# Softmax with tokens on partitions, turned by DMA, in a fused attention and bilinear FFN

## The chip, the cores and the metric

The kernel runs on one core of a Trainium2 chip. The metric is the device time in microseconds of one execution, the median of several. The core has five engines that this text names: TensorE (PE, matmuls), VectorE (DVE), ScalarE (ACT), GpSimd (POOL) and SyncE (SP), which here only issues DMAs. Each engine works through its own queue in order and waits on semaphores. DMAs issued by SP and those issued by GpSimd have queues of their own.

## What is computed

Eight batches of eight heads, 576 tokens (S), head dimension 64 (D), 32 memories (M) in each head:

```
a      = softmax(phi) over the 576 tokens' 32 memories      # [tokens, 32] of each head
k_m    = a.T @ k ;  v_m = a.T @ v                           # 32 x 64 means, each head
attn   = softmax(q @ k_m.T / 8) over the 32 memories        # [tokens, 32]
x      = attn @ v_m, heads side by side                     # [4608, 512]
out    = ((x @ w_a) * (x @ w_b)) @ w_out                    # d_ff = 1536, out [4608, 512] f32
```

The kernel leaves out maxima, folds `v_m` into `w_a` and `w_b` for each batch (`vab`), so that `attn` is the direct input of the up products, and works in f16 with f32 sums in PSUM. In place of dividing `a` by its sums it divides the means by sums taken with a column of ones.

## The kernel before, in words

Work is cut by batch. A batch has 12 blocks of d_ff (128 each) and two halves of 288 tokens. An *up step* for block `i` and half `hf` (`up_half`, L598) is two matmuls into a PSUM tile `pa` and two into `pb`, both with `attn[b]` (tile A, heads times memories on partitions, tokens along the row) as the moving side; ACT copies `pa` to `a_sb` (L609), DVE multiplies it with `pb` into `ht` (L612). The *down products* (`two_downs`, L464) take two blocks of 128 tokens at once by a scheme with seven products in place of eight, from sums of `ht` that GpSimd makes (`sum_tokens`, L455), into PSUM tiles `py`, `pv`, `px`; ACT and DVE finish them into `o_sb` (four buffers), and SP stores them.

The order is written out by hand. `ups` runs through the up steps and after each pulls some down products from a common list, at a rate that `Work.plan` sets from what is ready, and then runs one *slot* of a plan: names of units of the next batch, separated by blanks, several in one slot joined by `+`. A prime stands for the batch after that one, `_` for the one before. `d3` pulls three products at once, `L` starts the loads of a later batch on GpSimd's queue. The main loop (L703 to L710) takes batches b = 2 to 7; each has two halves of 12 slots, and the plan of its slots treats batch b + 1: `second` for b = 2, `every` for 3 to 5, `last` for 6. In this text "the loop of batch 4" is b = 4, in which batch 5's attention is made.

The units of a batch:
- `exp0`, `exp1`: exponential of phi (ACT).
- `kv`, `km` (or `km0`, `km1`): the sums with k, v and ones on TensorE into two PSUM tiles `pkv`, and their scaling into `rep` (`take_kv`, L233).
- `kvt` or `kvd`: turning `rep` into `kvT`, by six TensorE transposes and a DVE copy (`kv_transpose`, L241), or by one DMA transpose that SP issues (`kv_turn`, L247). Batches 2 to 4 use the first, 5 to 7 the second.
- `qt0` to `qt3`: turning the query in 32x32 blocks of f32 pairs on DVE (`q_transpose`, L203). The contraction over D is then split in even and odd columns, and each tile of TensorE has 32 rows.
- `sc`, `e0`, `e1`: scores (L297, memories on partitions) and their exponential into E (L310).
- `den0`, `den1`: sums over memories, a matmul with a block matrix of ones into `pD` (L320), and their logarithm L (ACT, L321).
- `nr0`, `nr1`: R = exp(-L) (ACT, L329) and A = E * R (GpSimd, L331).
- `v0` to `v2`, `x0a` to `x2b`: folds of the means into the weights (`fold`, L343) and their copies out of PSUM (`take_fold`, L355).

PSUM has eight banks. `Banks` hands them out in turn; tiles taken with `hold=True` (scores, folds, `py`, `pv`, `px`, `pkv`) keep theirs until freed, the others go round. Tiles of the pools `mid` and `inp` (E, A, qT, kvT, the query) have two buffers.

Of the kernel before, what the change touches and what calls it, by code (L numbers as in the profile page):

```python
# [18 lines left out]
def kernel(  # L19
# [26 lines left out]
    mid = ctx.enter_context(tc.tile_pool(name="mid", bufs=2))  # L46
    small = ctx.enter_context(tc.tile_pool(name="small", bufs=2))
# [25 lines left out]
    phis, qs, kvs = {}, {}, {}  # L73
# [71 lines left out]
    banks = Banks()  # L145
# [31 lines left out]

    attn = {}
    vabs = {}

    def head(g, j):

        jj = j ^ g
        return jj % 2, 2 * g + jj // 2

    def units(b):

        u = {}
        t = {}
# [10 lines left out]
        def q_transpose(hp):  # L200
            if hp == 0:
                t["qT"] = mid.tile([P, NHP, NI * D], F16, name="qT")
            nc.vector.transpose(out=t["qT"][:, hp, :].bitcast(F32), in_=qs[b][:, hp, :].bitcast(F32))  # L203

        def kv_sums():

            t["pkv"] = [banks.take([P, 3, D], F32, "pkv", hold=True) for _ in range(2)]
            for i in range(NI):
                for g in range(2):
                    for j in range(4):  # L210
                        r, hp = head(g, j)
                        nc.tensor.matmul(  # L212
                            t["pkv"][g][0][32 * j:32 * j + 32],
                            t["exp"][64 * r:64 * r + 64, hp, i, :],
                            kvs[b][64 * r:64 * r + 64, :, hp, D * i:D * (i + 1)],
                            start=(i == 0),
                            stop=(i == NI - 1),
                            tile_position=(64 * r, 32 * j),
                        )

        def take_kv(gs=range(2)):

            if gs[0] == 0:
                t["rep"] = mid.tile([P, 6, P], F16, name="rep")
                t["rphi"] = small.tile([P, 2], F32, name="rphi")
            for g in gs:
                pkv, bank = t["pkv"][g]
                nc.vector.reciprocal(out=t["rphi"][:, g:g + 1], in_=pkv[:, 2, 0:1])
                km = pkv[:, 0].rearrange("p (d e) -> p e d", e=2).unsqueeze(2).to_broadcast([P, 2, 4, 32])
                vm = pkv[:, 1].unsqueeze(1).to_broadcast([P, 2, D])  # L230
                for out, x in ((t["rep"][:, 2 * g:2 * g + 2].rearrange("p e (z d) -> p e z d", z=4), km),
                               (t["rep"][:, 4 + g].rearrange("p (z d) -> p z d", z=2), vm)):
                    nc.vector.tensor_scalar(out=out, in0=x, scalar1=t["rphi"][:, g:g + 1], scalar2=None, op0=ALU.mult)  # L233
                banks.free(bank)

# [8 lines left out]
        def kv_turn():  # L244

            t["kvT"] = mid.tile([P, 6, P], F16, name="kvT")
            nc.sync.dma_start_transpose(out=t["kvT"], in_=t["rep"].rearrange("p x d -> p (x d)"))  # L247

        def sums(g, x):

# [32 lines left out]
        def scores(gs):  # L283
# [7 lines left out]
            for dh in range(2):  # L291
                for z in range(2):
                    for g in gs:
                        for j in range(4):
# [8 lines left out]
                                tile_position=(row, 32 * j),  # L303
                            )

        def exp_scores(g):
            Ev = t["E"].rearrange("p g (i z s) -> p g i z s", z=2, s=32)
            for z in range(2):
                pss, bank = t["pss", g][z]
                nc.scalar.activation(out=Ev[:, g, :, z, :], in_=pss, func=AF.Exp, scale=1.0 / (8.0 * CS))  # L310
                banks.free(bank)
# [11 lines left out]
        def normalise(g, hfs=slice(0, 2)):  # L323
# [6 lines left out]
            engine = nc.vector if b < 2 else nc.gpsimd  # L330
            engine.tensor_tensor(out=attn[b][:, g, sl], in0=t["E"][:, g, sl], in1=t["R", g][:, sl], op=ALU.mult)  # L331

        def fold(lo, hi, zs):
            if b not in vabs:
                vabs[b] = [mid.tile([P, 2, d_ff], F16, name=f"vab{x}") for x in range(2)]
            if len(zs) > 1 and b > 2:
                work.settle()
            for z in zs:
                t["pva", lo, z] = [banks.take([P, 512], F32, "pva", hold=True) for _ in range(2)]
                for j in range(4):  # L340
                    for g in range(2):
                        r, hp = head(g, j)
                        nc.tensor.matmul(  # L343
                            t["pva", lo, z][g][0][32 * j:32 * j + 32, 0:hi - lo],
                            t["kvT"][64 * r:64 * r + 64, 4 + g, M * j:M * j + M],
                            w_sbs[z][64 * r:64 * r + 64, hp, lo:hi],
                            start=True,
                            stop=True,
                            tile_position=(64 * r, 32 * j),
                        )  # L350
# [7 lines left out]
        def one(f, *a):  # L358
            return lambda: f(*a)

        for z in range(2):
            u[f"exp{z}"] = one(exp_phi, z)
            u[f"ks{z}"] = one(sums, z, 0)
            u[f"kt{z}"] = one(transpose, z, 0)
            u[f"vs{z}"] = one(sums, z, 1)
            u[f"vt{z}"] = one(transpose, z, 1)
            u[f"s{z}"] = one(scores, (z,))
            u[f"e{z}"] = one(exp_scores, z)
            u[f"km{z}"] = one(take_kv, (z,))
            u[f"den{z}"] = one(denominators, z)  # L370
            u[f"nr{z}"] = one(normalise, z)
            for hf in range(2):
                u[f"den{z}{hf}"] = one(denominators, z, (hf,))
                u[f"nr{z}{hf}"] = one(normalise, z, slice(hf, hf + 1))
            for n in range(NCH):
                u[f"v{n}{'ab'[z]}"] = one(fold, 512 * n, 512 * (n + 1), (z,))
                u[f"x{n}{'ab'[z]}"] = one(take_fold, 512 * n, 512 * (n + 1), z)
            for n in range(2):
                u[f"hv{n}{'ab'[z]}"] = one(fold, 256 * n, 256 * (n + 1), (z,))
                u[f"hx{n}{'ab'[z]}"] = one(take_fold, 256 * n, 256 * (n + 1), z)  # L380
        for n in range(NCH):
            u[f"v{n}"] = one(fold, 512 * n, 512 * (n + 1), (0, 1))
        for x in range(4):
            u[f"qt{x}"] = one(q_transpose, x)
        u["sc"] = one(scores, (0, 1))
        u["kv"] = one(kv_sums)
        u["km"] = one(take_kv)
        u["kvt"] = one(kv_transpose)
        u["kvd"] = one(kv_turn)
        u["-"] = lambda: None  # L390
        return u
# [201 lines left out]
    work = Work()  # L593
# [57 lines left out]
    def slots(b, names):  # L651

        def both(fs):
            return lambda: [f() for f in fs]
        def unit(n):
            if n == "fin":
                return lambda: work.pull(-work.done % NFF)
            if n == "L":
                return lambda: load(b + 2) if b + 2 < B else None
            if n[0] == "y":  # L660
                return lambda: some(int(n[1:]))
            if n[0] == "d" and n[1:].isdigit():
# [34 lines left out]
    ups(half_steps(1, 0, 4), slots(1, "- v2a+x2a+v2b+x2b+qt0' - - qt1'+exp0' exp1'+qt2' - kv'+km'+y9"))  # L697
    work.plan(S + HALF, 10)
    ups(half_steps(1, 1, 4), slots(2, "qt3 kvt - sc+e0+e1 - den0+den1+nr0 - v0+nr1+x0a x0b - v1+x1b x1a"))
    second = "v2_+d1+x2a_+exp0 x2b_ exp1 - kv+km+d2 qt0 d4+kvt+qt1 - qt2+qt3+sc+e0 - e1+v0+d2+x0a+x0b den0+d3 exp0' v1+nr0+x1a x1b+qt0' L+d5 den1 v2+x2a exp1'+qt1'+x2b - - qt2'+kv'+nr1+km' - - qt3'+kvt'+d5"  # L700
    every = "- sc+e0 e1 den0 nr0+v0+x0a+x0b - - exp0' exp1' - v1+x1b+x1a+kv'+km0'+d3 - den1+km1' kvd'+qt0' - - nr1+qt1' v2+x2a+x2b - qt2' - qt3' - - L"
    last = "sc+e0 d3 - e1 v0+x0b - - den1 - - den0+d1 x0a+v1+x1b x1a+nr0 - - - v2+x2a - nr1 - - - - x2b"
    for b in range(2, B):  # L703
        if b == 2:
            load(4)
# [35 lines left out]
```

The softmax here doesn't subtract the row's maximum and nothing guards it: scores larger than these inputs give would overflow.

## Time and profile before

| | us |
|---|---|
| median of 3 runs | 241.4 (241.38 to 241.75) |
| the profiled execution | 241.3 |
| its span, first to last instruction | 239.6 |
| granted TensorE clock, mean | 0.997 |

The first 24 us or so are loading and the first batch; the loop of batch 2 begins at about 72 us, those of batches 4 and 5 at about 126 and 154, and after the last up step only down products are left.

The page's slices cut the span in 40 equal parts; a digit is the busy share in tenths:

```profile
PE   7958999999999999999999999999999999999993
DVE  4636784469949878966975659775976585756642
ACT  2266671669698599687776867797776877465330
POOL 7953244499979629981799948984769087937001
DMA  6999999999967954992359945599130303032155
```

The groups of instructions that the change touches (line, engine, operation, out<-in, shapes and count; then busy us and mean ns of one; then the idle time before them and what ended it):

```profile
L331 POOL TENSOR_TENSOR A<-E,R 128x576 f16<-128x576 f16 x12 | 15.3, 1278 | 4.3 <-ACT R L329 4.3
L310 ACT ACTIVATE E<-pscore 128x288 f16<-128x288 f32 x32 | 11.4, 419 | 11.4 <-PE pscore L297 11.2
L321 ACT ACTIVATE L<-pD 128x288 f32<-128x288 f32 x32 | 11.5, 418 | 6.0 <-PE pD L320 5.8
L203 DVE STREAM_TRANSPOSE qT<-q_sb 128x288 f32<-128x288 f32 x32 | 14.6, 464 | 0.3 <-DMA q_sb<-in_q_dram 0.3
L329 ACT ACTIVATE R<-L 128x576 f16<-128x576 f32 x14 | 9.8, 702 | 0.1
L233 DVE TENSOR_SCALAR rep<-pkv,rphi 128x256 f16<-128x256 f32 x12 | 5.8, 484 | 0.4
L233 DVE TENSOR_SCALAR rep<-pkv,rphi 128x128 f16<-128x128 f32 x12 | 4.1, 342 | 0.0
L455 POOL TENSOR_TENSOR h_sums<-ht 128x768 f16<-128x768 f16 x28 | 46.0, 1644 | 33.9 <-DVE ht L612 33.7
```

### The profile page before, as it was taken

How to read it: one execution, taken by the hardware profiler on the slowest of the kernel's cores; microseconds unless marked ns; L12 is line 12 of the kernel's file. 1: busy time of each engine (PE TensorE's matmuls, PEld its weight loads, DVE VectorE, ACT ScalarE, POOL GpSimd, SP SyncE). 2: the span in 40 equal slices, each digit the busy share in tenths (PEclk: the TensorE clock that was granted, in tenths of full speed). 3: DMA queues.
4: the chain of work that ended last, by engine and by line, in shares of the span. 5: the costliest groups of instructions: out<-in, count | busy, mean ns of one | idle time of the engine just before them, and what ended most of it. 6: DMA issues, size and time to landing. Idle time of an engine off the chain costs nothing.

```text
span 239.6 us, 7764 instructions
## 1 busy us (share of the span) xinstructions
PE 230.6 (96%) x3092; PEld 170.3 (71%) x3092; DVE 165.4 (69%) x403; ACT 158.7 (66%) x410; POOL 159.5 (67%) x135
## 2 busy tenths in 40 slices
PE   7958999999999999999999999999999999999993
PEld 7734664456757867878787787878787778888882
DVE  4636784469949878966975659775976585756642
ACT  2266671669698599687776867797776877465330
POOL 7953244499979629981799948984769087937001
PEclk9999999999999999999999999999999999999998
DMA  6999999999967954992359945599130303032155
GB/s 230 239 197 207 206 258 206 252 213 279 224 154 161 214 115 98 222 208 49 43 123 233 211 90 65 141 212 191 41 85 11 81 16 74 10 83 61 38 130 125
DMA packets 28164, 34.71 MB, mean 145 GB/s; under 512 B 4416, under 2 KB 22208, under 8 KB 28128
## 3 DMA queue, kind: packets, MB, share of 16 engines
q0 software_dynamic: 19264, 23.14, 52.2%
q1 hardware_dynamic: 8352, 10.29, 18.4%
q10 hardware_dynamic: 512, 0.79, 1.0%
q8 instruction: 24, 0.39, 0.7%
q14 instruction: 12, 0.10, 0.1%
HBM read 42.47 MB, written 9.44 MB: 217 GB/s over the span
## 4 chain that ended last, share of the span: by engine, by line
PE 77%; DMA 16%; DVE 2%; issue 1%; POOL 1%; ACT 1%; DVEq 0%; POOLq 0%
PE py L473 18%; PE pa L601 18%; PE pb L601 17%; PE pv L473 9%; DMA wb_sb<-in_moe_w_b_dram 6%; DMA q_sb<-in_q_dram 5%; PE pva L343 5%; DMA kv_sb<-in_v_dram 4%; PE px L473 4%; PE po L398 2%; PE pkv L212 2%; PE pscore L297 1%; PE pD L320 1%; DVE ht L612 1%; ACT a_sb L609 1%
## 5 line engine op out<-in xcount | busy, mean ns | idle before, releaser
L612 DVE TENSOR_TENSOR ht<-a_sb,pb 128x288 f16<-128x288 f16 x168 | 73.3, 450 | 37.5 <-ACT a_sb L609 26.8
L601 PEld LDWEIGHTS <-vab 128*128 128x128 f16 x768 | 72.4, 98 | 24.9 <-issue 7.8
L609 ACT CAST a_sb<-pa 128x288 f16<-128x288 f32 x168 | 66.7, 407 | 25.7 <-PE pa L601 24.6
L601 PE MATMUL pa<-A,vab 128*128 128x288 f16 x384 | 75.8, 287 | 0.1
L601 PE MATMUL pb<-A,vab 128*128 128x288 f16 x384 | 75.0, 286 | 0.7 <-ACT vab L355 0.5
L455 POOL TENSOR_TENSOR h_sums<-ht 128x768 f16<-128x768 f16 x28 | 46.0, 1644 | 33.9 <-DVE ht L612 33.7
L473 PEld LDWEIGHTS <-h_sums 128*128 128x128 f16 x384 | 37.0, 98 | 7.7 <-issue 1.1
L355 DVE CAST vab<-pva 128x512 f16<-128x512 f32 (+1 forms) x52 | 32.3, 644 | 4.8 <-PE pva L343 4.2
L355 ACT CAST vab<-pva 128x512 f16<-128x512 f32 (+1 forms) x52 | 27.7, 569 | 7.8 <-PE pva L343 7.2
L473 PEld LDWEIGHTS <-ht 128*128 128x128 f16 x288 | 28.1, 98 | 5.7 <-issue 0.4
L473 PE MATMUL py<-w_sums,h_sums 128*128 128x256 f16 x192 | 31.3, 273 | 0.0
L455 POOL TENSOR_TENSOR h_sums<-h_sums,ht 128x768 f16<-128x768 f16 x14 | 23.0, 1640 | 1.0
L455 POOL TENSOR_TENSOR h_sums<-ht,h_sums 128x768 f16<-128x768 f16 x14 | 23.0, 1642 | 0.9
L310 ACT ACTIVATE E<-pscore 128x288 f16<-128x288 f32 x32 | 11.4, 419 | 11.4 <-PE pscore L297 11.2
L331 POOL TENSOR_TENSOR A<-E,R 128x576 f16<-128x576 f16 x12 | 15.3, 1278 | 4.3 <-ACT R L329 4.3
L473 PE MATMUL py<-wo_sb,ht 128*128 128x256 f16 x96 | 16.7, 273 | 0.0
L473 PE MATMUL pv<-w_sums,h_sums 128*128 128x256 f16 x96 | 16.5, 273 | 0.0
L473 PE MATMUL py<-w_sums,ht 128*128 128x256 f16 x96 | 15.9, 272 | 0.1
L473 PE MATMUL px<-wo_sb,ht 128*128 128x256 f16 x96 | 15.9, 273 | 0.0
L321 ACT ACTIVATE L<-pD 128x288 f32<-128x288 f32 x32 | 11.5, 418 | 6.0 <-PE pD L320 5.8
L480 ACT ACTIVATE u<-py 128x256 f32<-128x256 f32 x32 | 12.5, 390 | 4.3 <-PE py L473 3.7
L203 DVE STREAM_TRANSPOSE qT<-q_sb 128x288 f32<-128x288 f32 x32 | 14.6, 464 | 0.3 <-DMA q_sb<-in_q_dram 0.3
(65 smaller groups left out, 275.7 us busy)
## 6 DMA issues: line engine op xcount, KB each, us to landing
out_dram<-o_sb SPq DMA_DIRECT2D x68, 128.0 KB, 2.4
phi_sb<-in_phi_dram POOLq DMA_DIRECT2D x8, 576.0 KB, 5.4
kv_sb<-in_v_dram POOLq DMA_DIRECT2D x7, 576.0 KB, 10.3
kv_sb<-in_k_dram POOLq DMA_DIRECT2D x7, 576.0 KB, 6.6
q_sb<-in_q_dram POOLq DMA_DIRECT2D x6, 576.0 KB, 13.1
wo_sb<-in_moe_w_out_dram POOLq DMA_DIRECT2D x6, 256.0 KB, 13.7
q_sb<-in_q_dram POOLq DMA_DIRECT2D x4, 288.0 KB, 9.7
wa_sb<-in_moe_w_a_dram POOLq DMA_DIRECT2D x2, 512.0 KB, 13.8
```

The source lines that it names most:

```text
L203: nc.vector.transpose(out=t["qT"][:, hp, :].bitcast(F32), in_=qs[b][:, hp, :].bitcast(F32))
L310: nc.scalar.activation(out=Ev[:, g, :, z, :], in_=pss, func=AF.Exp, scale=1.0 / (8.0 * CS))
L321: nc.scalar.activation(out=t["L", g][:, sl], in_=pD, func=AF.Ln)
L331: engine.tensor_tensor(out=attn[b][:, g, sl], in0=t["E"][:, g, sl], in1=t["R", g][:, sl], op=ALU.mult)
L343: nc.tensor.matmul(t["pva", lo, z][g][0][32 * j:32 * j + 32, 0:hi - lo], t["kvT"][64 * r:64 * r + 64, 4 + g, M * j:M * j + M], w_sbs[z][64 ...
L355: engine_copy(out=vabs[b][z][:, g, lo:hi], in_=pva[:, 0:hi - lo])
L455: engine.tensor_tensor(out=out, in0=in0, in1=in1, op=op)
L473: nc.tensor.matmul(po, lhs[:, i], rhs[:, i], start=first and i == 0, stop=i == KH - 1, skip_group_check=not first)
L480: nc.scalar.mul(out=x, in_=po, mul=scale)
L601: nc.tensor.matmul(ps, vabs[b][x][:, g, P * i:P * (i + 1)], attn[b][:, g, HALF * hf:HALF * (hf + 1)], start=(g == 0), stop=(g == 1))
L609: nc.scalar.copy(out=a_sbs[b, i, hf], in_=ps)
L612: nc.vector.tensor_tensor(out=ht[:, i, t0:t0 + HALF], in0=a_sbs.pop((b, i, hf)), in1=ps, op=ALU.mult)
```

## The change

For batches from `TURNED` = 3 on, the query is turned by one DMA transpose that SP issues (`q_turn`, 18 blocks of 128x128, f16), and the scores (`token_scores`) contract over all 64 columns of D in one matmul, on tiles of 64 rows: 16 matmuls in place of 32. `take_kv` writes keys and values of a group side by side with one scaling instead of two, and `kv_turn` turns four blocks instead of six; batches 3 and 4 use it now too.

For batches 4 to 7 the softmax over memories is done with tokens on partitions: SP turns E by a DMA transpose (`e_turn`, 9 blocks), DVE sums each run of 32 memories and takes the reciprocal (`token_sums`, in two parts of 640 and 512 columns), GpSimd multiplies the first part and DVE the second (`token_normalise`), and SP turns the result back into A (`a_turn`). The units `den` and `nr` of these batches go. Batch 3 keeps them.

The three plans are written anew.

```diff
+    TURNED = 3
+        def q_turn():
+            t["qT"] = mid.tile([P, NHP, NI * D], F16, name="qT")
+            nc.sync.dma_start_transpose(out=t["qT"].rearrange("p c f -> p (c f)").rearrange("p (n x) -> p n x", x=P),
+                                        in_=qs[b].rearrange("p c f -> p (c f)"))
...
+                if b >= TURNED:
+                    parts = ((t["rep"][:, 2 * g:2 * g + 2].rearrange("p x (z d) -> p x z d", z=2),
+                              pkv[:, 0:2].unsqueeze(2).to_broadcast([P, 2, 2, D])),)
...
-            nc.sync.dma_start_transpose(out=t["kvT"], in_=t["rep"].rearrange("p x d -> p (x d)"))
+            n = 4 if b >= TURNED else 6
+            nc.sync.dma_start_transpose(out=t["kvT"][:, 0:n], in_=t["rep"][:, 0:n].rearrange("p x d -> p (x d)"))
...
+        def token_scores():
...
+                t["pss", g] = [banks.take([P, 5 - y, 64], F32, "pscore", hold=True) for y in range(2)]
+            for g in range(2):
+                for x in range(2):
+                    for j in range(4):
+                        r, hp = head(g, j)
+                        y = (hp + x) % 2
+                        n = (NI * hp + y) // 2
+                        nc.tensor.matmul(
+                            t["pss", g][y][0][32 * j:32 * j + 32],
+                            t["kvT"][64 * x:64 * x + 64, 2 * g, M * j:M * j + M],
+                            qTv[64 * x:64 * x + 64, n:n + 5 - y, 64 * r:64 * r + 64],
+                            start=True,
+                            stop=True,
+                            tile_position=(64 * x, 32 * j),
+                        )
...
+        def e_turn():
+            t["ET"] = mid.tile([P, 2, S], F16, name="E").rearrange("p g s -> p (g s)").rearrange("p (n x) -> p n x", x=P)
+            nc.sync.dma_start_transpose(out=t["ET"], in_=t["E"].rearrange("p g s -> p (g s)"))
...
+            nc.vector.tensor_reduce(out=out, in_=blocks(x), axis=mybir.AxisListType.X, op=ALU.add)
+            nc.vector.reciprocal(out=out, in_=out)
...
+            engine = (nc.gpsimd, nc.vector)[x]
+            engine.tensor_tensor(out=blocks(x), in0=blocks(x), in1=sums.unsqueeze(2).to_broadcast(list(blocks(x).shape)),
+                                 op=ALU.mult)
+
+        def a_turn():
+            attn[b] = mid.tile([P, 2, S], F16, name="A")
+            nc.sync.dma_start_transpose(out=attn[b].rearrange("p g s -> p (g s)").rearrange("p (n x) -> p n x", x=P),
+                                        in_=t["ET"].rearrange("p n x -> p (n x)"))
...
-                            t["kvT"][64 * r:64 * r + 64, 4 + g, M * j:M * j + M],
+                            t["kvT"][64 * r:64 * r + 64, 2 * g + 1 if b >= TURNED else 4 + g, M * j:M * j + M],
...
-    second = "v2_+d1+x2a_+exp0 x2b_ exp1 - kv+km+d2 qt0 d4+kvt+qt1 - qt2+qt3+sc+e0 - e1+v0+d2+x0a+x0b den0+d3 exp0' v1+nr0+x1a x1b+qt0' L+d5 den1 v2+x2a exp1'+qt1'+x2b - - qt2'+kv'+nr1+km' - - qt3'+kvt'+d5"
-    every = "- sc+e0 e1 den0 nr0+v0+x0a+x0b - - exp0' exp1' - v1+x1b+x1a+kv'+km0'+d3 - den1+km1' kvd'+qt0' - - nr1+qt1' v2+x2a+x2b - qt2' - qt3' - - L"
-    last = "sc+e0 d3 - e1 v0+x0b - - den1 - - den0+d1 x0a+v1+x1b x1a+nr0 - - - v2+x2a - nr1 - - - - x2b"
+    second = "v2_+d1+exp0+x2a_ exp1+d6+x2b_ qd+kv+km0+km1+kvd - - d4 - - sc+e0 - e1+d3+v0+d2+x0a+x0b den0 - v1+nr0+x1a x1b+qd' L+exp0'+d5 - v2+x2a exp1'+x2b - - kv'+den1+nr1+km' kvd' - d7"
+    every = "sc+e0+e1+d3+ed+d3 - - v0+x0a+x0b - sm0 sm1 - tn1+exp0' d5+tn0+exp1' ad v1+x1b+x1a+kv'+km0' qd'+km1' kvd' - - v2+x2b - - - - - L+x2a"
+    last = "sc+e0+e1+ed - - v0+x0b+d5 - - sm0+d4 tn0 sm1+d5 tn1 x0a+v1+x1a+x1b - ad - - v2+x2a - - - d4 - x2b"
```

`qd`, `ed` and `ad` are the three turns, `sm` the sums and `tn` the normalisation by parts.

More of the change, by code (lines that the diff above doesn't have):

```diff
@@ L230, in take_kv @@
                 vm = pkv[:, 1].unsqueeze(1).to_broadcast([P, 2, D])
-                for out, x in ((t["rep"][:, 2 * g:2 * g + 2].rearrange("p e (z d) -> p e z d", z=4), km),
-                               (t["rep"][:, 4 + g].rearrange("p (z d) -> p z d", z=2), vm)):
+                parts = ((t["rep"][:, 2 * g:2 * g + 2].rearrange("p e (z d) -> p e z d", z=4), km),
+                         (t["rep"][:, 4 + g].rearrange("p (z d) -> p z d", z=2), vm))
+                if b >= TURNED:
+                    parts = ((t["rep"][:, 2 * g:2 * g + 2].rearrange("p x (z d) -> p x z d", z=2),
+                              pkv[:, 0:2].unsqueeze(2).to_broadcast([P, 2, 2, D])),)
+                for out, x in parts:
                     nc.vector.tensor_scalar(out=out, in0=x, scalar1=t["rphi"][:, g:g + 1], scalar2=None, op0=ALU.mult)
@@ L304, in scores, with token_exp_scores @@
                             )
+        def token_scores():
+            t["E"] = mid.tile([P, 2, S], F16, name="E")
+            work.settle()
+            qTv = t["qT"].rearrange("p c f -> p (c f)").rearrange("p (n x) -> p n x", x=P)
+            for g in range(2):
+                t["pss", g] = [banks.take([P, 5 - y, 64], F32, "pscore", hold=True) for y in range(2)]
+            for g in range(2):
+                for x in range(2):
[11 more added lines that the diff above has]
+                        )
+        def token_exp_scores(g):
+            Ev = t["E"].rearrange("p g (i s) -> p g i s", s=64)
+            for y in range(2):
+                pss, bank = t["pss", g][y]
+                nc.scalar.activation(out=Ev[:, g, y::2, :], in_=pss, func=AF.Exp, scale=1.0 / (8.0 * CS))
+                banks.free(bank)
         def exp_scores(g):
@@ L331, in normalise, with blocks, token_sums, token_normalise @@
             engine.tensor_tensor(out=attn[b][:, g, sl], in0=t["E"][:, g, sl], in1=t["R", g][:, sl], op=ALU.mult)
+        def e_turn():
+            t["ET"] = mid.tile([P, 2, S], F16, name="E").rearrange("p g s -> p (g s)").rearrange("p (n x) -> p n x", x=P)
+            nc.sync.dma_start_transpose(out=t["ET"], in_=t["E"].rearrange("p g s -> p (g s)"))
+        def blocks(x):
+            return t["ET"][:, slice(0, 5) if x == 0 else slice(5, 9)].rearrange("p n (j m) -> p (n j) m", m=M)
+        def token_sums(x):
+            if x == 0:
+                t["sum"] = small.tile([P, 36], F32, name="sum")
+            out = t["sum"][:, slice(0, 20) if x == 0 else slice(20, 36)]
+            nc.vector.tensor_reduce(out=out, in_=blocks(x), axis=mybir.AxisListType.X, op=ALU.add)
+            nc.vector.reciprocal(out=out, in_=out)
+        def token_normalise(x):
+            sums = t["sum"][:, slice(0, 20) if x == 0 else slice(20, 36)]
+            engine = (nc.gpsimd, nc.vector)[x]
[5 more added lines that the diff above has]
+                                        in_=t["ET"].rearrange("p n x -> p (n x)"))
         def fold(lo, hi, zs):
@@ L367, in units @@
             u[f"s{z}"] = one(scores, (z,))
-            u[f"e{z}"] = one(exp_scores, z)
+            u[f"e{z}"] = one(token_exp_scores if b >= TURNED else exp_scores, z)
             u[f"km{z}"] = one(take_kv, (z,))
@@ L384, in units @@
             u[f"qt{x}"] = one(q_transpose, x)
-        u["sc"] = one(scores, (0, 1))
+        u["sc"] = token_scores if b >= TURNED else one(scores, (0, 1))
+        u["qd"] = q_turn
+        u["ed"] = e_turn
+        for x in range(2):
+            u[f"sm{x}"] = one(token_sums, x)
+            u[f"tn{x}"] = one(token_normalise, x)
+        u["ad"] = a_turn
         u["kv"] = one(kv_sums)
```

## Prediction

> **What bounds the kernel now.** I read the page's busy shares first, then its slices, then the windows of the middle part, then TensorE's timeline.
>
> ```profile
> PE 230.6 (96%) x3092; PEld 170.3 (71%) x3092; DVE 165.4 (69%) x403; ACT 158.7 (66%) x410; POOL 159.5 (67%) x135
> ```
> ```profile
> 100.00:200.00 100.00, 100.00 (x1293) 77.47 (x1292) 73.30 (x176) 75.60 (x196) 73.33 (x52) 1.00 0.58 115
> 154.00:166.00 12.00, 12.00 (x149) 9.12 (x155) 7.21 (x18) 10.15 (x27) 9.13 (x7) 1.00 1.12 215
> 166.00:176.00 10.00, 10.00 (x174) 7.73 (x159) 9.71 (x25) 7.69 (x19) 6.71 (x5) 1.00 0.42 102
> ```
>
> After the stretch come its length and the busy us of PE, weight loads, DVE, ACT and POOL, then clock, DMA share and GB/s. TensorE is busy for all of 100 to 200 us; no other engine passes 78 there. A busy TensorE need not be at its pace, so I looked at starts:
>
> ```profile
> 157.47 0.49 PE L473 MATMUL px<-wo_sb,ht 128*128 128x256 f16 x3
> 157.80 0.41 PE L320 MATMUL pD<-E,ones 128*128 128x288 f16 x2
> 158.04 0.41 PE L601 MATMUL pa<-A,vab 128*128 128x288 f16 x2
> 158.29 0.41 PE L601 MATMUL pb<-A,vab 128*128 128x288 f16 x2
> ```
>
> Two 288-column matmuls start 0.24 us before the next pair, three 256-column ones take 0.33: 0.12 and 0.11 us each, and this pitch holds through the middle. So TensorE's instruction stream is the time. What leaves it is gained in full; what makes it wait is lost in full; ACT, DVE and POOL work that leaves is worth nothing by itself.
>
> **What the Trainium skill says.** "TensorEngine Tiling (Array Packing)", Available Configurations: 32x32 gives sixteen independent tiles, 64x32 eight. The trace agrees: sixteen 64x32 matmuls of 512 columns of a fold start within 0.44 us, thirty-two 32x32 ones of the scores within 0.40. "VectorE: DVE Perf Modes", The perf-mode tier table: a reduction runs at 1x only. No run here shows one; DVE's copies out of PSUM (256 columns 421 ns, 512 columns 684 ns) give 1.03 ns a column and 0.16 us fixed, which I take. "DMA: Bandwidth & Descriptors", Queues, rings and completion order: a DMA engine goes round its queues packet by packet, finishing a packet before it changes. The trace agrees in kind: four stores together move in 2.7 us alone (119.6 to 122.3 us), and in 4.4 us when GpSimd's loads run beside them (131.8 to 136.2, 527 load packets between 318 of the stores' queue).
>
> **What leaves TensorE.** Batches 4 to 7 lose the denominators: 4 matmuls of 288 columns each, 16 x 0.123 = 1.96 us. Batches 3 and 4 lose the transposes of the means:
>
> ```profile
> 80.30 0.50 PE L241 MATMUL pT<-ident,rep 128*128 128x128 f16 x6
> 80.63 0.41 PE L601 MATMUL pa<-A,vab 128*128 128x288 f16 x2
> ```
>
> 0.33 us each, 0.66 us. The scores of batches 3 to 7 go from 32 matmuls on sixteen tiles (two rounds of 288 columns) to 16 matmuls on eight tiles (two rounds of 320 or 256): the same columns, 0 us; bounds -0.1 and +0.1 us a batch. The folds only read another place. Sum: 2.6 us off 239.6. Without any new wait the profiled execution (241.3 us, 1.7 of it outside the span) would be 238.7.
>
> **What the other engines get.** DVE for each of batches 4 to 7 loses four stream transposes (4 x 0.464 = 1.86 us) and two of four scalings (2 x 0.342), and gets two reductions (0.16 + 640 x 1.03 ns = 0.82, and 0.69), two reciprocals (0.16 each) and one normalisation over 512 (0.69): 2.5 us for 2.5. But they move: the transposes stood in a batch's second half, the sums stand in its first. The windows show that DVE has room there: 7.21 of 12 us; with 2.5 more 81%. ACT loses 4 x 0.418 and 2 x 0.702 us a batch, hidden today, so nothing. POOL loses two of 1.278 and gets one over 640 columns: 768 take 1.64 and 576 take 1.28, so 1.4 us; with an f32 operand at most twice, 2.8. Equal or better, and nobody waits for it before the turn back.
>
> **The turns.** What TensorE will wait for is a DMA:
>
> ```profile
> L247 SPq DMA_TRANSPOSE kvT<-rep x3: 1211/1219/2083, 116.2 to 170.3; - x3
> DMA to landing us min/median/max: 2.7/3.3/3.7
> ```
>
> The one at 170.34 us takes SP 1.2 us to issue; its 768 pieces of 256 B start at 171.5, run 1.1 us and land 0.45 us later. By pieces: the means now have 512 (2.2 to 2.8 us), E and A 1152 (1.2 + 1.4 + 0.45 = 3.0; up to 4), a query 2304 (1.2 + 2.75 + 0.45 = 4.4; up to 7 if issue grows with size). All three old turns ran while no load did. For a turn beside loads there is no row; the bounds are no slowing, and twice the stores' loss, some 3.5 us on E's. I take the stores' own factor 4.4/2.7 on the moving part: E's 3.9 us, the means' 2.6.
>
> Which turns matter? SP goes on as soon as its data are there, whatever the slot, so a slot only sets the order.
>
> *Queries.* Batch 3's was loaded from 47.98 us on, at most 22.4 us to landing, so it is turned by about 71 to 76 us, and the scores come at some 82. Batches 4 to 7 wait for the query load (over by 167 us for batch 7), then behind A's turn, which waits for POOL and DVE. In the window from 154.8 us POOL would finish its four sums by 162, then normalise until about 164; A's turn and the next query's are on their way by 166 and landed by 172, the means' by 173; the scores come at about 178. Stores behind these waits have two pairs of o_sb. Nothing.
>
> *E.* Its scores start at time 0; the old trace has the first E 0.5 us later and four of them by 1.8. The turn lands at 4.8 alone, 5.7 by my choice, up to 9 at the bound. The reduction stands five slots on: five times 0.49 us of ups, about 18 products of 0.11, a fold 0.44 and the scores 0.4 make 5.2, and DVE comes 0.7 behind: 5.9. So it fits, by 0.2 us. If it does not, the ht products behind the reduction wait, and through their PSUM banks TensorE: six banks beside the held ones, three slots of 0.82 us, so DVE may stand 2.5 us first. Batches 5 and 6 are turned amid a load (124 to 137, 154 to 167 us in the old trace); batch 4's in the end of one (95.5 to 107); batch 7's meets none. I take 0.1 us.
>
> *Means.* Here the way is short. Batch 3: the loop's fold starts at 73.28 in the old timeline; two ups (0.49 each), ten products (1.1), the fold and the sums (0.87) put the sums' end at about 76.8. Two reciprocals and two scalings (2 x 0.16 + 2 x 0.484 us) give 78.4, the turn in the middle of a load (73.5 to 86.5 us) 81.0 by my choice, and TensorE reaches the scores, six ups and 21 products (5.2 us) later, at 82.0: nothing, bound 0.5. Batch 4: the old sums run from 96.73 to 97.6; scaled by 99.1, turned by 101.7 (load until 107). TensorE gets there through pD (0.25), two slots (0.82 each), the 7 products put in as cover (0.76) and an up with three products (0.82) at about 101.1: 0.6 us lost, bounds 0 and 1.5.
>
> *Batch 3's second normalisation.* The denominators go to the same slot as the normalisation. From 97.6: matmul 0.3, two Ln at 0.4, R 0.7, POOL 1.28 give 100.8; TensorE wants A at 100.3, after pD, the two slots and the cover. 0.5 us lost, bounds 0 and 1.5 (POOL in the middle of a sum of 1.64).
>
> *Placing.* The exponentials of both halves stand together, so ACT's copies of the next slot come 0.6 us later; six products cover it. One half of a fold's banks is held six slots longer, leaving four for the ups; the old last stage holds them so too and TensorE does not wait there. 0 to 0.2 a batch, I take 0.
>
> Sum of waits 0.1 + 0.6 + 0.5 = 1.2; 241.3 - 2.6 + 1.2 = 239.9 us. The profiled run stands 0.1 below the median of 241.4, less than I can resolve here; I leave it.
>
> **Rivals.**
> 1. *No new wait*: the 7 covering products and idle SP carry everything. For: the turns at their smallest fit. Against: the two waits around 100 us come out over zero with the measured durations. 238.7 us.
> 2. *A wash*: turns at the upper end of what was seen alone (3.7 us for six blocks), both waits at 1.0 to 1.5 us: waits equal the 2.6 us. 241.3 us.
> 3. *Turns starve beside loads* (the other side). Place: E's turn before the reduction on DVE for batches 4 to 6. A piece of 256 B is a small part of a packet round when load pieces of 1152 B stand between. It decides once E's turn takes over 6.5 us from issue: the 4.1 us to the reduction plus 2.5 us of banks. With the turn ending only when the load does, 9 to 10 us, each of the two batches amid loads loses 3 us, batch 4 about 1, the means of batches 3 and 4 another 1 each over my choice: 1.2 + 6 + 1 + 1 = about 9 at worst; half of that, 4.5 more than my forecast, is the likelier. 244.4 us. For: the stores' slowing; against: those turns need only a third of a load's bytes.
> That the change does not do what it says I exclude: the denominators, Ln and R are gone from the order of instructions of batches 4 to 7.
>
> **How the numbers follow.** Forecast 0.45, no new wait 0.12, wash 0.14, starving 0.29. A difference of 0.2%, 0.5 us, is what a measurement of this kernel can tell. Forecast and no wait lie below 240.9 but for a little of the forecast's upper end (0.02): faster 0.55. Same: the wash's 0.11 around 241.4. Slower: starving 0.29, and the rest, 0.34 in all. The range leaves out the upper half of the starving case and the edge of no wait: 238.6 to 244.0. The likeliest case alone spans 239.0 to 240.9.
>
> **What would show it.** Right: no pD for batches 4 to 7; TensorE's pitch unbroken from 104 us on, with small waits for A and for kvT around 100; E's turn landing within 4 us; the reduction not waiting for a DMA. Wrong: DVE idle before the reduction, released by a DMA, with TensorE waiting for ht behind it; turns of over 6 us beside loads; the scores waiting for qT; or the time at 242 and more with TensorE's matmuls as few as counted here.

## The result and the profile after

The changed kernel takes 260.7 us against 241.4 before: a ratio of 1.079 (95% interval 1.0766 to 1.0813). The forecast of 239.9 us was wrong, and so was its sign. The profiled execution took 260.1 us, with a span of 258.4 us, 18.8 more than before. One of the four executions took 278.2 us at a lower clock; it is left out of these figures, as is such an execution in experiment 1 (265.4 us).

From the page of the changed kernel: the busy shares, three rows of the 40 slices, and the chain of work that ended last, by engine and by line.

```profile
PE 233.4 (90%) x2984; PEld 170.0 (66%) x2984; DVE 164.8 (64%) x391; ACT 150.4 (58%) x386; POOL 154.5 (60%) x131
...
PE   8978999999999499469999959995999999999993
...
PEclk9999999999999889959999999999799999999999
DMA  6999999999889819983989929899552433030254
...
PE 79%; DMA 12%; DVE 3%; ACT 2%; issue 1%; SPq 0%; DVEq 0%
PE pa L671 18%; PE pb L671 17%; PE py L543 15%; PE pv L543 7%; DMA kvT<-rep 7%; PE pva L407 5%; PE po L468 4%; PE pw L151 4%; PE px L543 3%; DMA E<-E 3%; DMA out_dram<-o_sb 2%; PE pkv L218 2%; PE pk L271 1%; PE pscore L308 1%; DVE ht L682 1%
```

TensorE has 108 matmuls fewer (2984 for 3092), as the change intends, and yet stands: its row falls to 4, 5 or 6 in five slices of the middle, where it was 9 throughout before. The granted clock drops beside three of these places. In the chain, the turns of the means and of E alone make 10% of the span. The list of waits (who waited for whom: us in total, times, longest) names the same two:

```profile
PEld L329 <- DMA kvT<-rep: 10.2, 2, 5.9
...
PE pscore L329 <- DMA kvT<-rep: 9.6, 2, 5.6
...
DVE sum L383 <- DMA E<-E: 7.0, 2, 3.6
```

The first two lines are the same two stalls, seen by the weight loads and by the matmuls of the scores. TensorE's timeline (start, us, operation, in brackets the idle time before it and its releaser) shows the two stalls with the matmuls before them, and what follows the second:

```profile
82.58 0.82 PE L543 MATMUL pv<-wo_sb,h_sums 128*128 128x256 f16 x6
87.43 0.47 PE L329 MATMUL pscore<-qT,kvT 64*32 64x320 f16 x16 [4.03 <-DMA kvT<-rep]
...
105.83 0.38 PE L543 MATMUL py<-w_sums,h_sums 128*128 128x256 f16 x2
111.79 0.73 PE L329 MATMUL pscore<-qT,kvT 64*32 64x320 f16 x16 [5.58 <-DMA kvT<-rep]
...
113.71 0.69 PE L671 MATMUL pa<-A,vab 128*128 128x288 f16 x2
114.19 0.69 PE L671 MATMUL pb<-A,vab 128*128 128x288 f16 x2
```

The six matmuls from 82.58 us on start 0.11 us apart, so the last starts at 83.13, and from start to start the first stall is 4.30 us; the second is 5.85 in the same way. After the second, two 288-column matmuls start 0.48 us before the next pair, twice the 0.24 us of the kernel before: the clock is at half.

"TensorE: Matmul & The Clock Gate", Part 1: The HAM clock gate, in the Trainium skill says that TensorE falls to half rate after an idle window of some 3.4 us and is released after a busy window of that length. The trace agrees in part: half clock for 3.4, 6.8 and 3.4 us at three of the four long stalls, and none after the one of 3.6 us at 148 us. In the trace's clock records the changes (at 88.46, 91.88, 108.94, 115.77, 180.62 and 184.04 us) lie whole multiples of 3.41 us apart. Counted in such steps, the stall at 148 us leaves TensorE idle for 1.5 us of one step and 1.8 of the next; each of the other three stalls leaves it idle for at least 2.4 us of one. So a step need not be wholly idle for the clock to fall, and where a stall lies in the steps seems to decide as well as its length. That reading fits these traces; no run moved a stall to test it.

E's turns stop TensorE by way of DVE. From DVE's timeline, batch 5:

```profile
144.46 0.45 DVE L682 TENSOR_TENSOR ht<-a_sb,pb 128x288 f16<-128x288 f16 x1 [0.42 <-ACT a_sb L679]
148.32 0.82 DVE L383 TENSOR_REDUCE sum<-E 128x20 f32<-128x640 f16 x1 [3.41 <-DMA E<-E]
```

The reduction at the head of DVE's queue waits 3.41 us for E, with the `ht` and `o_sb` products queued behind it. TensorE's last start is at 148.11 us, and then it stands, in this case for a `py` bank whose `o_sb` product is in that queue:

```profile
147.78 0.60 PE L543 MATMUL px<-wo_sb,ht 128*128 128x256 f16 x4
151.67 0.49 PE L543 MATMUL py<-w_sums,ht 128*128 128x256 f16 x3 [3.29 <-DVE o_sb L554]
```

Batch 6 repeats this at 177, with TensorE waiting for an `ht` product.

The account, from start to start of TensorE's matmuls: stalls of 4.30 (batch 3's means), 5.85 (batch 4's), 3.56 and 3.46 us (E of batches 5 and 6) make 17.2, less 0.4 of usual pitch (four times 0.11), 16.8. Leaving out work saves 2.8 (experiment 2 below). What remains of 18.8 is 18.8 + 2.8 - 16.8 = 4.8 us, for the half clock: it was granted for 13.6 us, of which TensorE stood anyway for 2.9, so it can cost up to (13.6 - 2.9) / 2 = 5.4. That term is read from the trace; no run tested it by itself.

Why the turns were late shows at the tile kvT and at the line of E's turn, L374 (SP's issue min/median/max in ns, first and last start; then the time from the start of issue to landing):

```profile
L258 SPq DMA_TRANSPOSE kvT<-rep x5: 1194/1202/1482, 78.1 to 189.3; - x5
...
DMA to landing us min/median/max: 2.4/4.1/9.3
```
```profile
L374 SPq DMA_TRANSPOSE E<-E x4: 1282/1614/2029, 113.7 to 200.5; - x4
...
DMA to landing us min/median/max: 3.2/5.5/9.1
```

The smallest figures belong to turns that no load runs beside, the largest to those amid one. The DMA view of 82.5 to 85.0 us, when the means of batch 3 move (queue: packets, MB, share of the 16 engines' time; q0 is GpSimd's loads, q1 what SP issues):

```profile
q0 software_dynamic: 359, 0.40, 93.4%
q1 hardware_dynamic: 354, 0.09, 26.9%
```

The two queues pass in equal number, one piece of 256 B for one load packet of 1152 B. Counted by half microseconds, this holds through both late turns of the means: from 82.5 to 85.0 and from 108.0 to 111.0 us each half microsecond has 67 to 71 load packets and 67 to 79 pieces. A load packet occupies its engine 0.934 x 16 x 2.5 / 359 = 0.104 us, a piece 0.030, so most of the time is the load's.

### The profile page after: what moved, and what is told of

Same layout as the page of the kernel before. It is cut to its first block, busy times and chain, and to the rows that moved or that the text cites. A ratio compares the mean times of both kernels' runs of the same rounds, so it can differ in the third digit from the quotient of the medians.

```text
span 258.4 us, 7547 instructions
## 1 busy us (share of the span) xinstructions
PE 233.4 (90%) x2984; PEld 170.0 (66%) x2984; DVE 164.8 (64%) x391; ACT 150.4 (58%) x386; POOL 154.5 (60%) x131
## 4 chain that ended last, share of the span: by engine, by line
PE 79%; DMA 12%; DVE 3%; ACT 2%; issue 1%; SPq 0%; DVEq 0%
PE pa L671 18%; PE pb L671 17%; PE py L543 15%; PE pv L543 7%; DMA kvT<-rep 7%; PE pva L407 5%; PE po L468 4%; PE pw L151 4%; PE px L543 3%; DMA E<-E 3%; DMA out_dram<-o_sb 2%; PE pkv L218 2%; PE pk L271 1%; PE pscore L308 1%; DVE ht L682 1%
## 5 line engine op out<-in xcount | busy, mean ns | idle before, releaser
L671 PEld LDWEIGHTS <-vab 128*128 128x128 f16 x768 | 73.6, 99 | 29.6 <-issue 10.0
L671 PE MATMUL pa<-A,vab 128*128 128x288 f16 x384 | 77.4, 291 | 3.3 <-DVE ht L682 3.2
L671 PE MATMUL pb<-A,vab 128*128 128x288 f16 x384 | 76.2, 290 | 1.0 <-ACT vab L419 0.5
L543 PEld LDWEIGHTS <-h_sums 128*128 128x128 f16 x384 | 37.7, 99 | 9.7 <-issue 2.8
L419 ACT CAST vab<-pva 128x512 f16<-128x512 f32 (+1 forms) x52 | 28.1, 570 | 12.9 <-PE pva L407 12.9
L543 PE MATMUL py<-w_sums,ht 128*128 128x256 f16 x96 | 15.2, 272 | 3.4 <-DVE o_sb L554 3.3
L543 PE MATMUL pv<-w_sums,h_sums 128*128 128x256 f16 x96 | 16.8, 280 | 0.0
L543 PE MATMUL py<-wo_sb,ht 128*128 128x256 f16 x96 | 16.0, 273 | 0.0
L342 ACT ACTIVATE E<-pscore 128x320 f16<-128x320 f32 (+1 forms) x20 | 6.7, 415 | 13.2 <-PE pscore L329 13.2
L195 ACT ACTIVATE exp_sb<-phi_sb 128x576 f16<-128x576 f32 x16 | 10.9, 696 | 5.5 <-DMA phi_sb<-in_phi_dram 5.5
L389 POOL TENSOR_TENSOR E<-E,sum 128x640 f16<-128x640 f16 x4 | 5.1, 1264 | 14.7 <-PE py L543 8.5
L543 PE MATMUL pv<-wo_sb,h_sums 128*128 128x256 f16 x96 | 13.8, 273 | 0.0
```

What stands on the lines that cost most here:

```text
L195: nc.scalar.activation(out=t["exp"][:, 2 * z:2 * z + 2, :, :], in_=phis[b][:, 2 * z:2 * z + 2, :].rearrange("p c (i m) -> p c i m", m=M), ...
L342: nc.scalar.activation(out=Ev[:, g, y::2, :], in_=pss, func=AF.Exp, scale=1.0 / (8.0 * CS))
L419: engine_copy(out=vabs[b][z][:, g, lo:hi], in_=pva[:, 0:hi - lo])
L543: nc.tensor.matmul(po, lhs[:, i], rhs[:, i], start=first and i == 0, stop=i == KH - 1, skip_group_check=not first)
L671: nc.tensor.matmul(ps, vabs[b][x][:, g, P * i:P * (i + 1)], attn[b][:, g, HALF * hf:HALF * (hf + 1)], start=(g == 0), stop=(g == 1))
```

## The experiments

Line numbers in diffs of plans are left out; edits are against the changed kernel unless said otherwise.

**1. Means of batches 3 and 4 on TensorE again.** `kv_transpose` with four blocks, in place of the DMA, in the plan `second`:

```diff
+            n = 4 if b >= TURNED else 6
-            for x in range(6):
+            for x in range(n):
...
-    second = "v2_+d1+exp0+x2a_ exp1+d6+x2b_ qd+kv+km0+km1+kvd - - d4 - - sc+e0 - e1+d3+v0+d2+x0a+x0b den0 - v1+nr0+x1a x1b+qd' L+exp0'+d5 - v2+x2a exp1'+x2b - - kv'+den1+nr1+km' kvd' - d7"
+    second = "v2_+d1+exp0+x2a_ exp1+d6+x2b_ qd+kv+km0+km1 - - d4+kvt - - sc+e0 - e1+d3+v0+d2+x0a+x0b den0 - v1+nr0+x1a x1b+qd' L+exp0'+d5 - v2+x2a exp1'+x2b - - kv'+den1+nr1+km' - kvt' d7"
```

> Undoes one part: the means of batches 3 and 4 are turned on TensorE (four blocks each) and copied by DVE, as in the kernel before; all else is the changed kernel. Theory A (turns beside loads are late, and TensorE stands for them): the waits of 4.3 and 5.85 us for kvT go, and the half-clock stretches behind them (about 1.7 and 1.4 us), against 0.45 us for eight transposes: 260.7 - 12.8 = 248 us (247 to 249.5). Theory B (the new placing of units or SP's order loses the time, and kvT is only what is seen last): the waits come back elsewhere, 256 us or more.

Measured 251.1 us (250.7 to 253.0), ratio 1.042 (1.037 to 1.0465): between the two expectations. No stall for kvT is left, 10.2 us less, and the median falls by 9.6. What is still lost shows in the list of waits:

```profile
DVE sum L384 <- DMA E<-E: 9.5, 3, 4.5
```

DVE now waits for E three times, not twice. With the means in time, everything stands some 11 us earlier, and E's turn of batch 4, which had met no load (issued at 113.7, landed in 3.2 us), is issued at 102.35 beside the load of batch 5 and ends at 109. One late turn had shifted the next one out of the load's way. TensorE stalls 3.0, 1.8 and 4.4 us. At the first and the last the clock is at half for 3.4 us, so that a stall of 3.0 us (2.5 of it within one step of 3.41) was enough here. The span of 249.0 us is 12.2 over that of experiment 2: 8.8 are these stalls less the usual pitch, some 0.4 the eight transposes, and the 3.0 that remain are again near the most that the half clock can cost, 3.3.

**2. No loads after batch 3.** Batches 4 to 7 reuse the tiles of two batches before, so the turns stay and what runs beside them goes.

```diff
     def load(b):
+        if b > 3:
+            phis[b], qs[b], kvs[b] = phis[b - 2], qs[b - 2], kvs[b - 2]
+            return
```

> Leaves out the loads of batches 4 to 7 (they work on the inputs of batches 2 and 3 that lie in SBUF); turns, plans and all other work stay. Theory A: with no load in flight every turn lands in 2.5 to 5.8 us, the four waits go and with them the half clock: TensorE's own work alone, 239 us (238.5 to 240.5). Theory B (turns are slow because of stores, SP's order or their own size): at least the waits for E stay, 247 us or more.

Measured 238.6 us (238.52 to 238.67), ratio 0.988 (0.9866 to 0.9896), as expected. A window of its trace (length; busy us of PE, weight loads, DVE, ACT, POOL; clock, DMA share, GB/s), and the tile kvT:

```profile
100.00:200.00 100.00, 100.00 (x1230) 77.52 (x1229) 78.62 (x178) 68.79 (x179) 63.81 (x41) 1.00 0.50 94
```
```profile
L261 SPq DMA_TRANSPOSE kvT<-rep x5: 1189/1191/1212, 78.2 to 167.7; - x5
...
DMA to landing us min/median/max: 2.4/2.4/3.3
```

TensorE has no stall, the clock is full, and the means' turns take 2.4 us at the median where the longest took 9.3. The units, their slots, DVE's sums and normalisation are those of the changed kernel, so by themselves they cost nothing: the loss needs the loads. The span, 236.8, is 2.8 us under the kernel before, in whose middle TensorE had no stall either, so that this is work saved and not a wait of the loads.

**3. Sums and normalisation five to eight slots later**, and A's turn six, so that E may be late; the means still turned by DMA.

```diff
-    every = "sc+e0+e1+d3+ed+d3 - - v0+x0a+x0b - sm0 sm1 - tn1+exp0' d5+tn0+exp1' ad v1+x1b+x1a+kv'+km0' qd'+km1' kvd' - - v2+x2b - - - - - L+x2a"
+    every = "sc+e0+e1+d3+ed+d3 - - v0+x0a+x0b - - - - exp0' d5+exp1' - v1+x1b+x1a+kv'+km0' qd'+km1' kvd'+sm0 tn0+sm1 tn1 ad+v2+x2b - - - - - L+x2a"
```

> Moves one wait: in the loops of batches 3 to 5 the sums over ET stand eight slots later, and A's turn after the next query's and means' turns. Theory A: DVE no longer stands before the sums, so the waits of 3.56 and 3.46 us and one half-clock stretch of 1.7 us go, the two for kvT stay: 260.7 - 8.7 = 252 us (250.5 to 253.5). Theory B (DVE or POOL is overloaded by the sums and normalisations, the DMA only releases last): the loss stays at 258 us or more.

Measured 261.6 us, ratio 1.084 (1.082 to 1.0855): a miss for my own theory, though in the range of the other. DVE's wait for E is gone, as mine said, and that DVE is overloaded in the places of the changed kernel is excluded by experiment 2, where TensorE has no stall. But TensorE now stalls twice in each of three loops, by its timeline for `ht`, that is for banks that DVE has yet to read:

```profile
132.72 0.41 PE L407 MATMUL pva<-wb_sb,kvT 64*32 64x512 f16 x7 [0.73 <-DVE ht L682]
...
135.07 0.41 PE L671 MATMUL pa<-A,vab 128*128 128x288 f16 x2 [1.02 <-DVE ht L682]
```

1.11 and 1.29 us from start to start, 7.2 us in three loops: a new wait took the place of the one removed. In the new places DVE is indeed too busy, as experiments 4, 7 and 9 show.

**4. Edits 1 and 3 together.**

> The edits of e1 and e3 together. Theory A: no turn is late for its reader, so the gain of TensorE's work shows, less 0.45 us of transposes: 239.5 us (238.8 to 241). Theory B: 248 us or more.

Measured 246.1 us (246.08 to 246.19), ratio 1.019 (1.0177 to 1.0208): between the two expectations. No engine waits long for any turn, and the clock is full. The six stalls of experiment 3 are nearly all that is left (span 244.4, 7.6 over that of experiment 2; the stalls are 7.2, the eight transposes of the means some 0.4). DVE's and GpSimd's timelines show what stands before the larger one:

```profile
118.39 1.74 DVE L390 TENSOR_TENSOR E<-E,sum 128x512 f16<-128x512 f16 x1
```
```profile
117.94 1.64 POOL L526 TENSOR_TENSOR h_sums<-ht,h_sums 128x768 f16<-128x768 f16 x1
119.54 2.08 POOL L526 TENSOR_TENSOR h_sums<-ht 128x768 f16<-128x768 f16 x1
```

DVE's normalisation takes 1.74 us in three of four batches here, 0.68 in the changed kernel. It was issued inside a GpSimd sum and ended about 0.6 us after that sum; the next GpSimd sum then took 2.08 us in place of 1.64. "SBUF — State Buffer", SBUF: two separate sides, says that GpSimd and a DVE instruction with two inputs in SBUF share one pair of ports, which the first holds for its whole instruction while the other waits. The trace fits this to some 0.1 us: 119.58 + 0.68 = 120.26, and DVE was done at 120.13. Experiment 7 takes the instruction off DVE and the stall goes; whether 0.68 us in the same place would have cost TensorE anything was not tried.

**5. The loads moved instead.** Edit 1, the query first among a batch's loads, its turn earlier, and `L` in the fifth slot of `every` in place of the last:

```diff
     def load(b):
+        if b > 3:
+            load_q(b)
...
-        load_q(b)
+        if b <= 3:
+            load_q(b)
...
+    every = "sc+e0+e1+d3+ed+qd'+d3 - - v0+x0a+x0b L sm0 sm1 - tn1+exp0' d5+tn0+exp1' ad v1+x1b+x1a+kv'+km0' km1' kvd' - - v2+x2b - - - - - x2a"
```

In `second`, `qd'` stands with `e0` and `L` in the slot after it.

> The plans of e1 (means of batches 3 and 4 on TensorE) with the loads moved: those of batch 5 start six slots earlier in the loop of batch 2, those of batches 6 and 7 just after E's turn and not two slots before it; the query goes first among a batch's loads from batch 4 on, and its turn stands right behind E's. The sums keep their places. Theory A (the turns are late because load pieces stand between theirs): E's turns land within 4 us, DVE does not wait for them, 239.0 us (238.5 to 240.5). Theory B (E's turn is late for its place whatever the loads do): 247 us or more.

Measured 256.3 us, ratio 1.061 (1.058 to 1.063): a miss, in the range of the other theory but not for its reason. The loads of batches 4 and 5 now followed each other without a gap. SP's queue, and two of the waits:

```profile
82.30 12.92 SPq L211 DMA_TRANSPOSE qT<-q_sb  x1
```
```profile
DVE sum L387 <- DMA E<-E: 8.4, 1, 8.4
...
PE pscore L333 <- DMA qT<-q_sb: 4.6, 1, 4.6
```

A query is 2304 pieces; beside 1775 load packets they moved from 87.2 to 105.2 us, and SP was held 12.9 us by the issue alone, with all turns behind it. From 130 us on there was no stall: E's turns of batches 5 to 7 met no load, so E is late for its place only where a load meets it, and A's turn of batch 5, which did meet one and took 8.9 us to land, had no user waiting. Moving loads moves the collision unless the whole order leaves a gap.

**6. The kernel before, with turns that nobody reads.** Six turns of four blocks of E into a spare tile, two in each loop of `every`: once after `e1`, once after `qt0'`.

```diff
+        def idle_turn():
+            nc.sync.dma_start_transpose(out=warm.rearrange("p (n x) -> p n x", x=P), in_=t["E"][:, 0, 0:512])
```

> The kernel before with six more turns of four blocks (512 pieces of 256 B) into a tile that nobody reads, two in each of the loops of batches 3 to 5: one right after the second exponential, amid loads in the loops of batches 4 and 5, one behind the means' turn, with no loads. It measures the turn by itself. Theory A: amid loads the first piece comes 3.8 us after the issue and the landing after 8 to 9.5 us, against 1.2 and 2.4 us without; the time stays at 241.4 us (241.0 to 242.0), since nobody waits. Theory B (a turn is only slow where SP or its data are late): 2.2 to 3 us in both places. Theory C (transfers beside a turn suffer and cost by themselves): 243 us or more.

Measured 241.5 us, ratio 1.0011 (1.0003 to 1.0018). The tile of the spare turns, and the DMA view of 119.9 to 120.8 us, a turn with no load beside it:

```profile
L250 SPq DMA_TRANSPOSE warm<-E x6: 1190/1232/1980, 103.7 to 172.2; - x6
...
DMA to landing us min/median/max: 2.4/4.3/8.9
```
```profile
q1 hardware_dynamic: 540, 0.13, 71.8%
```

Alone, 512 pieces moved in 0.77 us (0.131 MB, 170 GB/s). In the two spare turns that lay wholly amid loads the first came 3.8 and 4.4 us after issue and the last 4.5 and 3.9 us later, about what the first theory said, and the time is as it said. So the slowing belongs to the pair of turn and load and needs nothing else of the changed kernel; and a late turn costs only by who waits for it.

**7. The edits of experiment 4 with the normalisation wholly on GpSimd**, to keep DVE clear of its sums.

```diff
-            engine = (nc.gpsimd, nc.vector)[x]
+            engine = nc.gpsimd
```

> e4 with the second part of the normalisation on GpSimd too. In e4 the DVE instruction took 1.74 us three times out of four beside a GpSimd sum, and 0.68 alone. Theory A (DVE is crowded in slots 11 to 16 by this instruction, and TensorE waits 2 x 1.2 us for the banks in each of three loops): most of the 6.7 us goes, 240.5 us (239.5 to 242.5). Theory B (DVE is crowded there without it): 244 us or more.

Measured 242.5 us, ratio 1.005 (1.0035 to 1.0067), on the upper edge of what was expected. The stalls of 1.29 us are gone, three of 1.11 stay, at the fold `v2`:

```profile
118.74 0.41 PE L408 MATMUL pva<-wb_sb,kvT 64*32 64x512 f16 x7 [0.73 <-DVE ht L683]
```

**8. Experiment 5 with the first `L` three slots later.**

> e5 with one slot name moved: the loads of batch 5 start in slot 12 of the loop of batch 2, so that those of batch 4 are over first and the query of batch 4 is turned between the two. In e5 that turn ran beside 1775 load packets for 18 us and held SP for 12.9 us. Theory A (every wait of e5 comes from that one turn): its loss of 17 us goes, E's turn of batch 4 meets the last 2 us of a load and lands within 5.5 us, no wait for a DMA on DVE or TensorE is left: 239.0 us (238.6 to 240.0), 1% below the kernel before. Theory B (E's turn of batch 4 stays late behind these loads, as in e1): a wait of 1.5 to 3 us near 107 us, 240.5 to 244 us.

Six executions spread from 242.0 to 258.2 us, so no ratio can be given: inconclusive as a time, and not the 239 expected. In the profiled execution (258.2) the next load met the turns of query 5 and of A:

```profile
132.39 0.66 PE L675 MATMUL pa<-A,vab 128*128 128x288 f16 x2 [6.90 <-DMA A<-E]
```

Why single executions differ so much was not tried; a turn that ends just before or just within a load is one reading.

**9. Edit 7 with the fold `v2` two slots later**, apart from `ad`.

```diff
-    every = "sc+e0+e1+d3+ed+d3 - - v0+x0a+x0b - - - - exp0' d5+exp1' - v1+x1b+x1a+kv'+km0' qd'+km1' kvd'+sm0 tn0+sm1 tn1 ad+v2+x2b - - - - - L+x2a"
+    every = "sc+e0+e1+d3+ed+d3 - - v0+x0a+x0b - - - - exp0' d5+exp1' - v1+x1b+x1a+kv'+km0' qd'+km1' kvd'+sm0 tn0+sm1 tn1 ad - v2+x2b - - - L+x2a"
```

> e7 with one unit moved: in the loops of batches 3 to 5 the last fold stands two slots later. In e7 TensorE waits there 3 x 1.1 us for a PSUM bank that DVE still holds, because DVE has the fold's copy, the means' scalings and both sums in the five slots before it; with two slots more DVE has caught up. Theory A (this is all that is left in e7): 242.5 - 2.5 = 240.0 us (239.3 to 240.8), faster than the kernel before. Theory B (the wait only moves to another bank): 242 us or more.

Measured 240.6 us, ratio 0.9965 (0.9952 to 0.9979): as expected, 20 us under the changed kernel and just under the kernel before. The window of its profiled execution:

```profile
100.00:200.00 100.00, 98.03 (x1203) 74.81 (x1201) 73.68 (x172) 65.84 (x171) 73.14 (x53) 1.00 0.83 155
```

Left are stalls of 0.65 and 1.26 us for A's turn and three of 0.5 us. That execution, 242.7 us, is the longest of seven: it has the clock at half for some of 14 to 22 us, in the loading at the start, which the others, with a mean clock of 0.996 to 1.000, lack. So the stalls listed here need not be those of a typical execution. The profiled execution of experiment 7 (242.8 us) has the same stretch, and two of its four take 242.2 us, so some 0.3 us of the step from experiment 7 to this one may be no gain of the edit.

## Why the prediction was wrong

*What failed.* One step: "For a turn beside loads there is no row; the bounds are no slowing, and twice the stores' loss ... I take the stores' own factor 4.4/2.7 on the moving part: E's 3.9 us, the means' 2.6." Measured, E's turns of batches 5 and 6 took 9.1 and 7.8 us, and the means' of batches 3 and 4 took 9.3 and 8.0. The stores were the wrong nearest row, for two reasons. A factor on the moving part supposes that the queues share by bytes or time; in these traces they pass packet for packet, so how much a turn loses depends on how small its pieces are. And the factor left the start alone, where 2.6 us are lost: beside loads the first piece comes 3.8 us after issue in place of 1.2. The larger bound failed too: twice the stores' loss put E's turn at 6.5 us, and the means' waits at no more than 0.5 and 1.5 us. They were 4.3 and 5.85.

The late start weighed nearly as much as the sharing. E's turn of batch 5 met only the end of a load (279 load packets between its first and its last piece), and it still took 5.9 us more than one alone: 2.7 from the late start, 3.2 in the moving.

*What the skill's page was worth.* "DMA: Bandwidth & Descriptors", Queues, rings and completion order, gave the right picture, queues served in turn. It speaks of some 9 to 17 descriptors in a packet; in what this trace lists as packets, one 256 B piece passes for one load packet (354 and 359). I had the picture and priced it by another transfer. The 16 engines make 359 / 16 = 22 such rounds in 2.5 us, 0.11 us each, and 512 pieces are 32 rounds: 3.6 us (3.8 and 4.5 measured).

*Means.* The starting point held: the means of batch 3 were foreseen as scaled at 78.4 and their turn was issued at 78.14, in the load as said. With 2.4 us, as in experiment 2, both waits (0 and 0.6 foreseen) are 0.2 us at most. (The terms given for batch 3 sum to 78.1, not 78.4.)

*E.* That "it fits, by 0.2 us" was true only of a turn alone (experiment 2), and the sum had no such margin: at the rate of its own row, 768 pieces in 1.1 us, E's 1152 take 1.65 us and not 1.4 (alone they took 1.53), which with the factor makes 0.4 us more. "DVE may stand 2.5 us first" was true as a delay: TensorE stopped 3.2 us after DVE did. But nothing was absorbed: DVE came out owing two reductions and two reciprocals (2.0 us) and all the queued products, and TensorE lost 3.56 us for 3.41 of waiting. The slack that hides a wait must also hold the work behind it.

*The clock* was not in the sum at all: some 4.8 us, a fifth of the loss of 21.6.

*What held.* TensorE's saving: 2.6 foreseen, 2.8 in experiment 2. DVE: reductions 0.82 and 0.67 us (0.82 and 0.69), normalisation 0.68 (0.69), reciprocals 0.28 and 0.25 (0.16). GpSimd's normalisation 1.26 (1.4). Queries: turned in 4.7 to 6.7 us (4.4 to 7), with no wait. The second normalisation of batch 3 (0.5 foreseen) shows no stall in experiment 2.

*The rivals.* The third had the mechanism, piece by piece, and the place of half of the stalls. It was priced at 244.4 because it halved its worst case, gave the means 1 us each and had no clock. Even that worst case, about 9 us, is under half of 21.6: E's two waits, 7.0 us, came near the 6 it allowed them, the means', 10.2, did not. The case of no new wait, 238.7, is what experiment 2 gives without loads.

*How much each part cost*, by medians: 260.7 as changed; 251.1 with the means off the DMA; 246.1 with E's users later as well; 242.5 with DVE off GpSimd's ports; 240.6 with one fold moved; 238.6 without loads. Edit 3 alone gained nothing and after edit 1 gained 5.0: the stalls it makes (7.2 us) about equal those that it removes until the means are in time, too, and batch 4's E would be late. That reading fits the sizes; it rests on sums of stalls.

## What to carry to other kernels

Before a step on the path is given to a DMA, list what is in flight when it will be issued: here a transposing DMA of small pieces started late beside a load, then advanced one piece for one packet of the load, and took up to four times as long as alone. Either keep the loads away from it for its whole length, or put its first user so late that the slowest landing seen in a trace still fits. Where one engine is busy all the time, price each stall in full, with the backlog that forms behind it and the clock it may cost, and look again after each repair, since every instruction then meets other transfers.

## What the runs showed of the hardware

- A DMA transpose of 512 pieces of 256 B landed in 2.4 us alone and in up to 9.3 beside loads; its pieces alternated one for one with load packets of 1152 B, and the first came 2.6 us later than alone. Why it comes later stayed open.
- Issuing a transpose can hold SP: 1.2 us for 4 blocks, 1.3 for 9 and 2.8 for 18 alone, up to 12.9 for 18 when issued amid loads (experiment 5).
- A DVE multiplication of two SBUF inputs over 512 columns took 1.74 us in place of 0.68 when it was issued during a GpSimd sum (experiment 4).
- TensorE's clock went to half for 3.4 or 6.8 us around stalls of 3.0 to 5.9 us (changed kernel and experiment 1), though not after one of 3.56; stalls of 1.1 to 1.8 us left it full (experiments 1 and 4). Its changes lay multiples of 3.41 us apart.
